# A gated recurrence and a multiplicative FFN on one core: single PSUM banks for the first up product, and a new order

## The chip, the core and the metric

The kernel runs on one core of a Trainium2 chip. The metric is the device time of one execution in microseconds; the median of five runs is given. Five engines matter here: TensorE (PE in the profile; its weight loads are PEld), VectorE (DVE), ScalarE (ACT), GpSimd (POOL), and SyncE (SP), whose queue issues the DMAs. Each takes its instructions in the order in which the program gives them; between engines, semaphores keep the order.

## What is computed

```python
# x, r_gate, i_gate: (4, 5824, 256) f32; a_param: (256,)
a_base = sigmoid(a_param)
a_t    = exp(8 * sigmoid(r_gate) * log(a_base))
norm   = sqrt(max(1 - a_t * a_t, 1e-6))
xg     = norm * sigmoid(i_gate) * x
for t in range(S):                   # a linear recurrence along the sequence
    h = a_t[:, t] * h + xg[:, t]
    y[:, t] = h
# then, over the 23296 rows of y:
out = ((y @ w1) * (y @ w2)) @ w3 @ w_out     # w1, w2: 256x1024, w3: 1024x1024, w_out: 1024x256
```

## The kernel before

The 23296 rows are cut into chunks (`sizes`: one of 256 rows, then 45 of 512). Of each chunk the kernel does the following steps; the letter is the step's name in the string `ORDER`.

- `r`, `i`, `x`: loads, on SP's queue (`load`, L121). `R`, `I`: tanh of half the gates on ACT (L130 or L132, L139), since a sigmoid is (1 + tanh)/2.
- `p`, `t`: (1 + tanh_i) times x on POOL (L144, L160), or fused on DVE (L158).
- `V`, `U`: the r gate and the product u are turned, channels onto partitions: by TensorE with an identity for the chunks in `TURN_R` and `TURN_U` (`turn_pe`, L167, result in PSUM), by a transposing DMA on SP's queue for the others (`turn_dma`, L177).
- `d`, `s`, `q`, `g`: the decay a = exp(...) on ACT in two halves (L188), its square on POOL or DVE (L195), the root on ACT (L199; it needs another activation table than tanh and exp, hence ACT_TABLE_LOAD), and the gating on DVE (L207, L210).
- `h`, `y`: the recurrence, as a hardware scan on DVE per half of the channels (L225), and its cast to bf16 on POOL or DVE (L233).
- `a`, `b`: the two up products on TensorE (`up`, L246). One step `a` makes 256 of the 1024 hidden columns for the chunk's rows: two output groups of 128, one PSUM bank each, held as one tile of two banks. `c`: ACT or DVE copies the tile pa to bf16 in SBUF (L252, L254). `m`: DVE multiplies that copy by pb, which it reads in PSUM (L266).
- `D`: the down product of 128 rows (L277). w3 and w_out were folded into one 1024x256 matrix at the start (`Ft`, `Fc`, `Fm`, `Fe`, L328 to L372). `e`: the output tile, two `D` together, is copied out of PSUM by ACT or DVE (L252, L254). `o`: it is stored, on SP's queue (L296, L292).

[...] `psum` holds three tiles of two banks, which pa and pb take in turn (tag `pab`). `psum_o` holds two single banks, for output tiles, turned gates and folding (tag `po`). A new tile waits for the last reader of the tile whose place it takes.

What runs when is written out by hand in one string: 2037 words such as `a9.3` (step `a`, chunk 9, part 3). A loop at the end of the kernel calls the steps in that order, and each engine's queue is the part of the string that falls to it. Gates run several chunks ahead of the products. Sets of chunk numbers choose the engine of a step that several could do: `DV_COPY`, `DV_EVAC`, `DV_SQUARE`, `DV_CAST`, `DV_TIMES` put it on DVE.

Of the kernel before, what the change touches and what calls it, by code (L numbers as in the profile page):

```python
# [22 lines left out]
def kernel(  # L23
# [26 lines left out]
    sizes = [256] + [CT] * 45  # L50
# [10 lines left out]
    psum = ctx.enter_context(tc.tile_pool(name="psum", bufs=3, space=bass.MemoryType.PSUM))  # L61
    psum_o = ctx.enter_context(tc.tile_pool(name="psum_o", bufs=2, space=bass.MemoryType.PSUM))
# [5 lines left out]
    la4 = consts.tile([P, NCB], F32, tag="la4")  # L68
    zz, zd, zt = (consts.tile([P, NCB], F32, name=tag, tag=tag) for tag in ("zz", "zd", "zt"))
# [9 lines left out]
    TURN_R = {0, 1, 2, 3, 4, 5, 7, 8, 13}  # L79
    TURN_U = {0, 1, 2, 3, 5, 8, 9}  # L80
    DV_TIMES = {0, 1, 2, 8}
    DV_PLUS = set()
    DV_HALF = set()
    DV_SQUARE = {(0, 0), (0, 1), (1, 0), (1, 1), (5, 0), (6, 0), (7, 1), (9, 1), (11, 0), (12, 0), (14, 0), (15, 1),
        (20, 1), (24, 1), (27, 0), (29, 0), (36, 0), (37, 0), (38, 0), (41, 0)}
    DV_CAST = {0, 20, 28, 37, 39, 40, 42, 45}
    DV_COPY = {(0, 3), (1, 1), (1, 3), (2, 1), (3, 2), (7, 2), (8, 0), (8, 1), (10, 0), (11, 1), (13, 0), (14, 0),
        (14, 2), (15, 3), (18, 1), (18, 3), (19, 3), (20, 3), (21, 3), (22, 3), (23, 1), (25, 0), (25, 2), (28, 1), (33,
        1), (33, 2), (36, 3), (40, 2), (41, 2), (41, 3), (44, 0), (45, 0)}
    DV_EVAC = {(0, 0), (1, 1), (2, 0), (2, 1), (3, 0), (4, 0), (4, 1), (5, 0), (6, 1), (7, 1), (8, 1), (9, 1), (10,  # L90
        0), (17, 0), (18, 1), (19, 0), (19, 1), (22, 0), (23, 1), (27, 0), (27, 1), (28, 1), (30, 0), (31, 0), (33, 1),
        (34, 1), (35, 0), (35, 1), (41, 1), (42, 0), (42, 1)}
    FOLD_ACT = {('c', 7), ('e', 0), ('e', 1), ('e', 4), ('e', 6), ('e', 7)}
    W_ACT = {('w2', 0), ('w3', 1), ('w3', 2), ('w3', 3)}
    W_DVE = {('w3', 0)}
    STAGE = {'w1': ['a', 'a'], 'w2': ['nrm', 'nrm'], 'wo': ['a', 'nrm'], 'w3': ['a', 'nrm', 'a', 'nrm', 'a', 'nrm',
        'a', 'nrm']}
    WARM = [30, 30, 24]
    src = {"r": rf, "i": jf, "x": xf}

    def flat(t):
        return t.rearrange("p cb j q -> p (cb j q)").rearrange("p (j d) -> p j d", d=D)

# [22 lines left out]
    def tanh_r(c):  # L126
        n = sizes[c] // P
        t = gates.tile([P, NCB, 4, P], BF16, name="th_r", tag="th_r")
        if c in TURN_R:
            nc.scalar.activation(out=flat(t)[:, :n, :], in_=T["r", c][:, :n, :], func=AF.Tanh, scale=0.5)  # L130
        else:
            nc.scalar.activation(out=t.rearrange("p cb j q -> p j cb q"), in_=cut(T["r", c]),  # L132
                                 func=AF.Tanh, scale=0.5)
        T["thr", c] = t
# [7 lines left out]
    def plus(c):  # L142
        t = T["thi", c]
        (nc.vector if c in DV_PLUS else nc.gpsimd).tensor_scalar(t, t, 1.0, 1.0, op0=ALU.add, op1=ALU.mult)  # L144

    def times(c, half):
# [5 lines left out]
        js = slice(0, n) if fused else slice(2 * half, 2 * half + 2)  # L152
        if c in TURN_U:
            u, t, xt = flat(u)[:, js, :], t[:, js, :], xt[:, js, :]
        else:
            u, t, xt = u.rearrange("p cb j q -> p j cb q")[:, js], cut(t)[:, js], cut(xt)[:, js]
        if fused:
            nc.vector.scalar_tensor_tensor(out=u, in0=t, scalar=1.0, in1=xt, op0=ALU.add, op1=ALU.mult)  # L158
# [15 lines left out]
    def turn_dma(c, key, nm):  # L174
        pool, tag = (gates, "rt") if key == "pr" else (held, "ut")
        dst = pool.tile([P, NCB, 4, P], BF16, name=tag, tag=tag)
        nc.sync.dma_start_transpose(out=dst.rearrange("p cb j q -> p (cb j) q"),  # L177
                                    in_=T[nm, c].rearrange("p cb j q -> p (cb j q)"))
        T[key, c] = dst.rearrange("p cb j q -> p cb (j q)")
# [10 lines left out]
    def square(c, cb):  # L190
# [3 lines left out]
        eng = nc.vector if (c, cb) in DV_SQUARE else nc.gpsimd  # L194
        eng.tensor_mul(out=T["n", c][:, cb, :w], in0=T["a", c][:, cb, :w], in1=T["a", c][:, cb, :w])  # L195
# [18 lines left out]
    def scan(c, cb):  # L214
# [3 lines left out]
        cuts = [0] + [b * S - starts[c] for b in range(1, B) if 0 < b * S - starts[c] < w] + [w]  # L218
        for lo, hi in zip(cuts[:-1], cuts[1:]):
            if (starts[c] + lo) % S == 0:  # L220
                init = 0.0
            else:
                pw = sizes[c - 1]
                init = T["h", c - 1][:, cb, pw - 1:pw]
            nc.vector.tensor_tensor_scan(  # L225
                T["h", c][:, cb, lo:hi], T["a", c][:, cb, lo:hi], T["n", c][:, cb, lo:hi],
                init, ALU.mult, ALU.add)

    def cast(c):
        w = sizes[c]  # L230
        T["y", c] = ypool.tile([P, NCB, CT], BF16, name="y_t", tag="y", bufs=4)
        eng = nc.vector if c in DV_CAST else nc.gpsimd
        eng.tensor_copy(out=T["y", c][:, :, :w], in_=T["h", c][:, :, :w])  # L233

    def warm(i):
        pp = psum.tile([P, 2, CT], F32, name="warm", tag="pab")
# [3 lines left out]
    def up(c, mp, nm, w_sb):  # L240
        w = sizes[c]
        pp = psum.tile([P, 2, CT], F32, name=nm, tag="pab")
        for q in range(2):
            m = 2 * mp + q
            for cb in range(NCB):
                nc.tensor.matmul(out=pp[:, q, :w], lhsT=w_sb[:, cb, m * P:(m + 1) * P],  # L246
                                 rhs=T["y", c][:, cb, :w], start=(cb == 0), stop=(cb == NCB - 1))
        T[nm, c, mp] = pp
# [7 lines left out]
    def copy(c, mp):  # L256
        w = sizes[c]
        sa = ffn.tile([P, 2, CT], BF16, name="sa", tag="sa")
        copy_to((c, mp) in DV_COPY, sa[:, :, :w], T["pa", c, mp][:, :, :w])
        T["sa", c, mp] = sa  # L260
# [54 lines left out]
    def load_w(nm, i):  # L315
        T["wf", nm, i] = held.tile([P, NCB, CT], F32, name="wf", tag=STAGE[nm][i])
# [31 lines left out]

    def rates_abs():
        nc.vector.scalar_tensor_tensor(out=zz, in0=la4, scalar=-1.0, in1=la4, op0=ALU.mult, op1=ALU.min)  # L350
# [23 lines left out]
    def last(c):  # L374
# [8 lines left out]
        "a": lambda c, mp: up(c, mp, "pa", w1_sb), "b": lambda c, mp: up(c, mp, "pb", w2_sb),  # L383
# [8 lines left out]
        "W": warm, "E": cast_ident, "A0.": rates_abs, "A1.": rates_exp, "A2.": rates,  # L392
# [3 lines left out]
        A0. r1 r0 i0 Lw3.0 x0 i1 A1. E R1 R0 x1 V0 V1 Lw1.1 Cw1.1 I0 A2. d0.0 d0.1 d1.0 d1.1 r2 Lw1.0 Lw2.0 Lw2.1 W1  # L396
        I1 s0.0 Cw3.0 s0.1 t0.1 s1.0 s1.1 W0 U0 i2 Cw1.0 q0 t1.1 g0 h0.0 q1 R2 U1 Lw3.1 h0.1 y0 W2 a0.2 g1 h1.0 c0.2
        V2 x2 h1.1 Lwo.1 Cw2.1 Cw2.0 Lwo.0 Ft0 a0.0 r4 a0.1 d2.0 c0.0 Lw3.2 c0.1 r3 b0.0 b0.1 s2.0 m0.0 m0.1 I2 d2.1
        Lw3.5 y1 Fc0 b0.2 b0.3 m0.2 s2.1 Lw3.4 a0.3 c0.3 m0.3 Cw3.1 Cwo.1 a1.2 Ft1 q2 a1.0 t2.1 Cwo.0 U2 i3 a1.1 c1.2
        b1.0 Fc1 c1.0 g2 c1.1 h2.0 R4 h2.1 m1.0 Lw3.3 Fm1 Fm0 Fe1 Fe0 y2 i4 b1.1 Cw3.5 r6 V4 b1.2 m1.1 m1.2 R3 V3 d4.0  # L400
        d4.1 a1.3 Ft5 d3.0 b1.3 a2.0 d3.1 Cw3.2 Fc5 x3 Ft2 c1.3 s4.0 Cw3.4 s4.1 I3 Lw3.6 Lw3.7 r5 s3.0 x4 s3.1 c2.0
        Fc2 p3 t3.0 I4 Cw3.3 Fm5 R6 i5 t3.1 b2.0 m1.3 Fe5 Cw3.6 p4 Fm2 q3 Ft4 a2.2 Fe2 m2.0 Ft3 Fc4 Fc3 a2.1 c2.1 Fm4
        U3 q4 Fe4 g3 a2.3 c2.2 Fm3 Ft6 r7 R5 Fe3 b2.1 Fc6 Cw3.7 Ft7 V6 r9 Fm6 b2.2 m2.1 Fc7 Fe6 c2.3 Fm7 V5 b2.3 x5
        t4.0 t4.1 I5 U4 Fe7 h3.0 h3.1 D1.0 d5.0 d5.1 R7 D1.1 m2.2 e1.0 y3 R9 m2.3 i6 i7 a3.0 g4 D0.0 h4.0 V7 a3.1 h4.1
        a3.2 p5 d6.0 c3.0 c3.1 d7.0 x6 d7.1 V9 r8 b3.0 I6 D0.1 s5.0 d9.0 d9.1 c3.2 y4 m3.0 e0.0 b3.1 d6.1 R8 b3.2 a4.0
        D1.2 r11 D1.3 m3.1 m3.2 s7.0 a4.1 s5.1 t5.0 p6 t5.1 e1.1 s6.0 c4.0 b4.0 s6.1 U5 s7.1 c4.1 I7 b4.1 o1.0 m4.0
        m4.1 q5 D2.0 D2.1 i8 e2.0 a4.2 a3.3 a4.3 q6 c4.2 b4.2 g5 c3.3 r10 r12 D2.2 b4.3 c4.3 b3.3 q7 h5.0 t6.0 p7 D2.3
# [121 lines left out]
```

## Time and profile before

| | us |
|---|---|
| median of 5 runs | 521.53 (519.48 to 522.41) |
| the profiled execution | 519.48 |
| its span | 517.7 |
| TensorE busy | 500.6 |
| VectorE busy | 476.6 |
| ScalarE busy | 429.5 |
| GpSimd busy | 298.4 |

The profile records one execution. Its span runs from the first to the last recorded instruction; the execution's own time is a little longer. A row of a group gives source line, engine, operation, the tiles written and read with shape and type, the count, the busy time, the mean of one in nanoseconds, and behind the second bar the idle time of the engine just before those instructions with what ended it. A row of the timeline begins with start and duration in microseconds; brackets hold the idle time before it and its releaser. Durations of neighbours on one engine can overlap, so the distance between starts is what the next instruction feels. Ends of matmuls are modelled.

### The profile page before, as it was taken

Reading aid. Unit: us, or ns where it says so; the run is one execution under the profiler, and the core shown is the slowest. Engines: PE = TensorE matmul, PEld = TensorE weight load, DVE = VectorE, ACT = ScalarE, POOL = GpSimd, SP = SyncE. Lnnn points to the kernel's source line nnn. Section 1 sums busy time; section 2 is a strip of 40 time slices with the busy share of each in tenths; the row PEclk is TensorE's granted clock in tenths of the full one; section 3 lists DMA queues with packets and bytes.
Section 4 is the critical chain, followed back from the end, with each engine's and each line's share of the span. In section 5 each row is a group of like instructions: output and inputs, shape, how many; then the busy total and the mean of one; then the engine's idle time right before and its main releaser. Section 6 shows DMA issues by size and latency. Waiting matters only on the chain.

```text
span 517.7 us, 8827 instructions
## 1 busy us (share of the span) xinstructions
PE 500.6 (97%) x3260; PEld 308.4 (60%) x3260; DVE 476.6 (92%) x456; ACT 429.5 (83%) x493; POOL 298.4 (58%) x251
## 2 busy tenths in 40 slices
PE   4799999999999999999999999999999999999997
PEld 4567666556565665566665556556556565566555
DVE  4998999999999999899999899999998998999973
ACT  6999998998898988999987997988977797766432
POOL 0677755777828765876566755757357756624000
PEclk9999999999999999999999999999999999999999
DMA  8999989899998876999879978998866978343113
GB/s 298 405 410 311 352 255 255 273 268 275 336 321 205 225 228 186 299 247 302 242 229 296 245 211 220 300 232 241 245 178 210 266 222 205 101 123 83 61 55 109
DMA packets 174604, 123.28 MB, mean 238 GB/s; under 512 B 84448, under 2 KB 170208, under 8 KB 174560
## 3 DMA queue, kind: packets, MB, share of 16 engines
q1 hardware_dynamic: 174288, 122.71, 82.3%
q8 instruction: 25, 0.41, 0.3%
q14 instruction: 19, 0.16, 0.1%
q10 hardware_dynamic: 272, 0.00, 0.0%
HBM read 78.91 MB, written 23.86 MB: 199 GB/s over the span
## 4 chain that ended last, share of the span: by engine, by line
PE 78%; DVE 12%; DMA 4%; issue 4%; POOL 1%; ACT 0%; SPq 0%; DVEq 0%; ACTq 0%; POOLq 0%
PE pb L246 26%; PE po L277 25%; PE pa L246 25%; DVE g_t L266 5%; DVE h_t L225 3%; DMA wf<-in_moe_w_dram 3%; PE pw L342 1%; DVE sa L252 1%; DVE nrm L210 1%; DMA out_dram<-ot 1%; PE ptr L167 1%; PE ptw L331 1%; DVE ot L252 0%; POOL y_t L233 0%; DVE nrm L195 0%
## 5 line engine op out<-in xcount | busy, mean ns | idle before, releaser
L246 PEld LDWEIGHTS <-w_sb 128*128 128x128 bf16 x1472 | 143.0, 98 | 149.8 <-issue 9.3
L266 DVE TENSOR_TENSOR g_t<-sa,pb 128x1024 bf16<-128x1024 bf16 (+1 forms) x184 | 216.0, 1199 | 16.9 <-PE pb L246 12.3
L254 ACT CAST sa<-pa 128x1024 bf16<-128x1024 f32 (+1 forms) x152 | 149.5, 1003 | 50.7 <-PE pa L246 47.3
L246 PE MATMUL pa<-y_t,w_sb 128*128 128x512 bf16 (+1 forms) x736 | 180.4, 377 | 3.1 <-DVE y_t L233 1.2
L246 PE MATMUL pb<-y_t,w_sb 128*128 128x512 bf16 (+1 forms) x736 | 180.1, 377 | 3.2 <-DVE sa L252 1.3
L277 PE MATMUL po<-wp_sb,g_t 128*128 128x256 bf16 x1456 | 179.4, 273 | 0.0
L277 PEld LDWEIGHTS <-g_t 128*128 128x128 bf16 x1456 | 142.3, 98 | 42.5 <-issue 0.2
L225 DVE TENSOR_TENSOR_SCAN h_t<-a_t,h_t,nrm 128x512 f32<-128x512 f32 (+3 forms) x90 | 116.6, 1321 | 1.2
L160 POOL TENSOR_TENSOR u_t<-th_i,x_t 128x512 bf16<-128x512 f32 x84 | 113.6, 1369 | 1.7 <-DMA ut<-u_t 0.8
L233 POOL CAST y_t<-h_t 128x1024 bf16<-128x1024 f32 x38 | 44.4, 1169 | 117.7 <-DVE h_t L225 101.1
L195 POOL TENSOR_TENSOR nrm<-a_t 128x512 f32<-128x512 f32 x72 | 85.0, 1193 | 18.2 <-ACT a_t L188 18.1
L144 POOL TENSOR_SCALAR th_i<-th_i 128x1024 f32<-128x1024 f32 x42 | 48.1, 1148 | 30.7 <-ACT th_i L139 30.7
L188 ACT ACTIVATE a_t<-rt,la 128x512 f32<-128x512 bf16 x74 | 59.1, 818 | 2.6 <-DMA rt<-th_r 1.5
L139 ACT ACTIVATE th_i<-i_t 128x1024 f32<-128x1024 f32 (+1 forms) x46 | 48.3, 1052 | 8.0 <-DMA i_t<-in_i_gate_dram 5.1
L210 DVE SCALAR_TENSOR_TENSOR nrm<-nrm,ut 128x1024 f32<-128x1024 f32 x39 | 52.7, 1354 | 0.7 <-DMA ut<-u_t 0.7
L254 ACT COPY ot<-po 128x512 f32<-128x512 f32 (+1 forms) x60 | 34.6, 577 | 17.2 <-PE po L277 16.2
L199 ACT ACTIVATE nrm<-nrm 128x1024 f32<-128x1024 f32 (+1 forms) x46 | 46.9, 1048 | 0.3
L252 DVE CAST sa<-pa 128x1024 bf16<-128x1024 f32 (+1 forms) x32 | 38.3, 1197 | 5.6 <-PE pa L246 5.4
L132 ACT ACTIVATE th_r<-r_t 128x1024 bf16<-128x1024 f32 x37 | 39.2, 1060 | 0.1
L199 ACT ACT_TABLE_LOAD x20 | 25.7, 1283 | 1.6 <-DVE nrm L195 1.3
L252 DVE COPY ot<-po 128x512 f32<-128x512 f32 (+1 forms) x33 | 21.9, 665 | 4.0 <-PE po L277 4.0
L195 DVE TENSOR_TENSOR nrm<-a_t 128x512 f32<-128x512 f32 (+1 forms) x20 | 17.7, 892 | 0.9 <-ACT a_t L188 0.9
(51 smaller groups left out, 153.3 us busy)
## 6 DMA issues: line engine op xcount, KB each, us to landing
r_t<-in_r_gate_dram SPq DMA_DIRECT2D x45, 512.0 KB, 5.7
i_t<-in_i_gate_dram SPq DMA_DIRECT2D x45, 512.0 KB, 5.3
x_t<-in_x_dram SPq DMA_DIRECT2D x45, 512.0 KB, 5.4
out_dram<-ot SPq DMA_DIRECT2D x89, 256.0 KB, 3.4
wf<-in_moe_w_dram SPq DMA_DIRECT2D x12, 512.0 KB, 9.2
wf<-in_moe_w_out_dram SPq DMA_DIRECT2D x2, 512.0 KB, 10.3
ut<-u_t SPq DMA_TRANSPOSE x39, 4.9
rt<-th_r SPq DMA_TRANSPOSE x37, 4.4
```

The costliest lines, as they stand in the source:

```text
L139: nc.scalar.activation(out=t[:, :n, :], in_=T["i", c][:, :n, :], func=AF.Tanh, scale=0.5)
L160: (nc.vector if (c, half) in DV_HALF else nc.gpsimd).tensor_mul(out=u, in0=t, in1=xt)
L188: nc.scalar.activation(out=a, in_=pr, func=AF.Exp, scale=la4[:, cb:cb + 1], bias=la4[:, cb:cb + 1])
L195: eng.tensor_mul(out=T["n", c][:, cb, :w], in0=T["a", c][:, cb, :w], in1=T["a", c][:, cb, :w])
L199: nc.scalar.activation(out=T["n", c][:, :, :w], in_=T["n", c][:, :, :w], func=AF.Sqrt, scale=-1.0, bias=1.0)
L210: nc.vector.scalar_tensor_tensor(out=T["n", c][:, :, :w], in0=T["n", c][:, :, :w], scalar=1e-3, in1=T["pu", c][:, :, :w], op0=ALU.max, op1 ...
L225: nc.vector.tensor_tensor_scan(T["h", c][:, cb, lo:hi], T["a", c][:, cb, lo:hi], T["n", c][:, cb, lo:hi], init, ALU.mult, ALU.add)
L246: nc.tensor.matmul(out=pp[:, q, :w], lhsT=w_sb[:, cb, m * P:(m + 1) * P], rhs=T["y", c][:, cb, :w], start=(cb == 0), stop=(cb == NCB - 1))
L252: nc.vector.tensor_copy(out=dst, in_=src_ps)
L254: nc.scalar.copy(out=dst, in_=src_ps)
L266: nc.vector.tensor_mul(out=T["g", c][:, 2 * mp:2 * mp + 2, :w], in0=T["sa", c, mp][:, :, :w], in1=T["pb", c, mp][:, :, :w])
L277: nc.tensor.matmul(out=po, lhsT=T["g", c][:, k, j * P:(j + 1) * P], rhs=wp_sb[:, k, :], start=(k == 0), stop=(k == KD - 1), skip_group_che ...
```

## The change

- **PSUM.** pb keeps tiles of two banks, now two of them in a pool of its own. pa becomes a tile of one bank, made and copied in two steps (`a9.3.0`, `a9.3.1`, `c9.3.0`, `c9.3.1`). It shares a ring of four single banks with the output tiles, the turned gates and the folding.
- **Copies.** A copy of pa is 512 columns wide instead of 1024. The product `m` still reads both halves at once.
- **Chunks.** Two chunks of 256 rows at the start, 44 of 512, one of 256 at the end (`dense` keeps small chunks contiguous for the transposing DMA).
- **Scans.** A scan that crosses a batch boundary was cut in two. Now the decay is set to zero at the boundary (`memset`) and one scan runs over it.
- **Engines.** The sets are new: squares may go to ACT (`AC_SQUARE`), casts too (`AC_CAST`); after chunk 10 all copies of pa and after chunk 9 all output copies but one of the last chunk's are on ACT. `TURN_R` and `TURN_U` are smaller.
- **Head.** a_param is loaded as two rows and turned by TensorE (`A3.`); warm-up matmuls (`W`) are regrouped.
- **Order.** A new string of 2452 words.

```diff
-    sizes = [256] + [CT] * 45
+    sizes = [256, 256] + [CT] * 44 + [256]
...
-    psum = ctx.enter_context(tc.tile_pool(name="psum", bufs=3, space=bass.MemoryType.PSUM))
-    psum_o = ctx.enter_context(tc.tile_pool(name="psum_o", bufs=2, space=bass.MemoryType.PSUM))
+    psum_b = ctx.enter_context(tc.tile_pool(name="psum_b", bufs=2, space=bass.MemoryType.PSUM))
+    psum_o = ctx.enter_context(tc.tile_pool(name="psum_o", bufs=4, space=bass.MemoryType.PSUM))
...
-    TURN_R = {0, 1, 2, 3, 4, 5, 7, 8, 13}
-    TURN_U = {0, 1, 2, 3, 5, 8, 9}
+    TURN_R = {0, 1, 2, 3, 4, 7, 12}
+    TURN_U = {0, 1, 2, 3, 6}
...
+    AC_SQUARE = {(1, 0), (2, 0), (3, 0), (4, 1), (7, 0), (10, 0), (11, 0), (12, 1), (13, 0), (13, 1), (14, 0), (14,
+        1), (15, 1)}
+    AC_CAST = {4}
+    DV_EVAC = {(5, 0), (9, 0), (9, 1)}
...
+        if (c, cb) in AC_SQUARE:
+            nc.scalar.activation(out=n, in_=a, func=AF.Square)
...
-        cuts = [0] + [b * S - starts[c] for b in range(1, B) if 0 < b * S - starts[c] < w] + [w]
-        for lo, hi in zip(cuts[:-1], cuts[1:]):
...
+        if cb == 0:
+            for b in range(1, B):
+                if 0 < b * S - starts[c] < w:
+                    nc.vector.memset(a[:, :, b * S - starts[c]:b * S - starts[c] + 1], 0.0)
...
+        nc.vector.tensor_tensor_scan(h[:, cb, :], a[:, cb, :], n[:, cb, :], init, ALU.mult, ALU.add)
...
-    def up(c, mp, nm, w_sb):
-        w = sizes[c]
-        pp = psum.tile([P, 2, CT], F32, name=nm, tag="pab")
+    def up(c, m, dst, w_sb):
+        w = sizes[c]
+        for cb in range(NCB):
+            nc.tensor.matmul(out=dst[:, :w], lhsT=w_sb[:, cb, m * P:(m + 1) * P],
+                             rhs=T["y", c][:, cb, :w], start=(cb == 0), stop=(cb == NCB - 1))
+
+    def up_a(c, mp, q):
+        T["pa", c, mp, q] = pp = psum_o.tile([P, CT], F32, name="pa", tag="po")
+        up(c, 2 * mp + q, pp, w1_sb)
+
+    def up_b(c, mp):
+        T["pb", c, mp] = pp = psum_b.tile([P, 2, CT], F32, name="pb", tag="pb")
         for q in range(2):
...
+            up(c, 2 * mp + q, pp[:, q, :], w2_sb)
...
-    def copy(c, mp):
-        w = sizes[c]
-        sa = ffn.tile([P, 2, CT], BF16, name="sa", tag="sa")
-        copy_to((c, mp) in DV_COPY, sa[:, :, :w], T["pa", c, mp][:, :, :w])
-        T["sa", c, mp] = sa
+    def copy(c, mp, q):
+        w = sizes[c]
+        if q == 0:
+            T["sa", c, mp] = ffn.tile([P, 2, CT], BF16, name="sa", tag="sa")
+        copy_to((c, mp, q) in DV_COPY, T["sa", c, mp][:, q, :w], T["pa", c, mp, q][:, :w])
...
+    def rates_turn():
+        pt = psum_b.tile([P, 2, CT], F32, name="pr_la", tag="pb")
+        nc.tensor.matmul(out=pt[:, 0, :NCB], lhsT=la_rows, rhs=ident_f[:NCB, :NCB], is_transpose=True,
+                         start=True, stop=True)
+        T["la"] = pt[:, 0, :NCB]
```

A stretch of the old order, and then one of the new:

```
D7.0 s12.1 r18 U13 o6.1 V16 I15 g11 D7.1 e7.0 r17 s14.0 m9.1 D7.2 b9.2 p12 s13.1 t12.0 t12.1
```

```
c11.2.0 q13 a11.1.0 q15 c11.1.0 b11.1 b11.0 g13 y12 a11.1.1 a11.2.1 D10.0 D10.1 D10.2 D10.3 c11.1.1 t16.0 a11.3.0
```

## The prediction

> **What bounds the kernel now.** I read the page first, then the three busy engines by stages of 20 us, then TensorE's timeline for its gaps, then ScalarE's for the pitch of its copies.
>
> ```profile
> PE 500.6 (97%) x3260; PEld 308.4 (60%) x3260; DVE 476.6 (92%) x456; ACT 429.5 (83%) x493; POOL 298.4 (58%) x251
> PEclk9999999999999999999999999999999999999999
> L254 ACT CAST sa<-pa 128x1024 bf16<-128x1024 f32 (+1 forms) x152 | 149.5, 1003 | 50.7 <-PE pa L246 47.3
> L254 ACT COPY ot<-po 128x512 f32<-128x512 f32 (+1 forms) x60 | 34.6, 577 | 17.2 <-PE po L277 16.2
> ```
>
> A busy PE need not be PE at its peak, so the 97% decides nothing; the starts in the timeline do:
>
> ```profile
> 16.33 0.60 PE L246 MATMUL pa<-y_t,w_sb 128*128 128x256 bf16 x4 [1.24 <-DVE y_t L233]
> 22.74 1.02 PE L246 MATMUL pa<-y_t,w_sb 128*128 128x512 bf16 x4 [0.62 <-POOL y_t L233]
> ...
> 309.04 1.02 PE L246 MATMUL pa<-y_t,w_sb 128*128 128x512 bf16 x4 [0.61 <-DVE g_t L266]
> 376.80 1.02 PE L246 MATMUL pb<-y_t,w_sb 128*128 128x512 bf16 x4 [1.25 <-DVE sa L252]
> ...
> 482.24 1.03 PE L246 MATMUL pa<-y_t,w_sb 128*128 128x512 bf16 x4
> 483.10 1.04 PE L277 MATMUL po<-wp_sb,g_t 128*128 128x256 bf16 x8
> 483.97 1.03 PE L246 MATMUL pb<-y_t,w_sb 128*128 128x512 bf16 x4
> 507.36 7.15 PE L277 MATMUL po<-wp_sb,g_t 128*128 128x256 bf16 x64
> ```
>
> From 482.24 to 483.10 and to 483.97: four matmuls of 512 columns take 0.866 us of PE, eight of 256 take 0.871. Eight turning matmuls of 128 take 0.445 (first starts of neighbouring groups). The program's useful work is then: first and second up product 315.3 (360 full half-chunk steps of 0.866 and 8 small of 0.436), down product 182 x 0.871 = 158.5, folding 10.6, turned gates 6.7: 491.1 us. The last matmul ends at 514.35 (507.36+7.15, less the 0.16 by which a group's end stands over the next start). So PE loses 23.3 us: 15.0 before 16.33 (1.3 of turns taken off), 2.3 from there to 22.74, and 6.0 later, in some ten gaps that end on VectorE (the two above are the largest). After PE's end come 3.3 us to the span's 517.7.
>
> ```profile
> 0.00:20.00 20.00, 10.98 (x142) 10.05 (x143) 12.97 (x31) 14.99 (x20) 3.88 (x9) 1.00 0.91 338
> 20.00:40.00 20.00, 19.14 (x159) 12.38 (x158) 19.34 (x24) 19.93 (x24) 16.00 (x16) 1.00 1.04 405
> 40.00:60.00 20.00, 19.97 (x157) 13.55 (x156) 18.38 (x21) 19.96 (x27) 13.08 (x12) 1.00 1.12 311
> 200.00:220.00 20.00, 19.80 (x118) 11.31 (x116) 18.34 (x16) 19.07 (x23) 15.37 (x14) 1.00 0.77 222
> 440.00:460.00 20.00, 20.00 (x123) 11.80 (x121) 19.13 (x17) 13.20 (x18) 12.55 (x10) 1.00 0.42 119
> ```
>
> Columns after the length: PE, weight loads, DVE, ACT, POOL. ACT is full from 20 to 60 us, having been idle 5.1 us before 60 (20-14.99, 0.07, 0.04). Later it has slack and DVE hasn't. So TensorE is the bound, and what can be won is 6 us of late gaps, a little head and the turns. ACT's place just behind it in the first 60 us matters for this change.
>
> **The change part by part.**
>
> *Fewer turns.* TURN_R and TURN_U shrink; with two chunks of 256 the turns cost 8 x 0.445 + 4 x 0.22 = 4.4 instead of 6.7. PE's work becomes 488.8: -2.3, all on the bound. In exchange there are 6 more transposing DMAs (82 for 76) on SP's queue, and three more loads. Transposes are late now for 1.5 (ACT on rt) and 0.7 us (DVE on ut) in all, as they are issued chunks ahead; cover gone, 1 us each.
>
> *Smaller banks.* pa is a single bank, four in a ring with po; pb keeps two doubles. Now PE's next product waits for the third tile back of pa and pb alike (fill 0.87, then DVE 1.14 or ACT 0.9). After it, a late DVE blocks only a later pb and a late ACT only the fourth single tile back, some 4 us of PE work. I expect most of the 6.0 us that end on DVE to go; what is late next is ACT. A PE group that waits for its bank holds every later matmul, the turns for ACT's own next decay among them.
>
> *Split copies and work moved from DVE to ACT.* By start-to-start times of neighbours ACT's 1024-column copy costs 0.91 us, a 512-column one 0.48 (ot, mean 0.487 of 42; sa of 512, 0.47 of 3). A pair costs 0.96: +0.05, 9 us over 184 pairs, not the 0.15 that the durations (2 x 577 - 1003) suggest. ACT's copies go from 149 full and 3 small ones to 324 and 11, its output copies from 60 to 88, and it takes 13 squares (not shown before: between 0.48, a copy, and 0.72, the decay of 512; I take 0.62) and one cast. Table loads fall from 40 to 34 behind the first (x 1.29). ACT: 420 -> 458 us. DVE loses 20 full copies' worth of time, 29 output copies, 15 squares and 7 casts: 461 -> 417. Uncut scans: the six pairs of pieces cost 10.8 us in the page's group of 90 against 6 x 1.35 = 8.1, and three memsets of two columns cost 0.2 each by the smallest DVE rows: -2 us of DVE, hidden. SP holds an output store until its copy is done; loads and transposes queue behind it, as they already do. POOL gains 9 us and has 200 to spare. The rates' turn adds one matmul and one DVE copy (0.2 by the small rows) ahead of the first exponential; a wait for the loads hides both, and uncovered they cost 0.5.
>
> *The new order.* Here the sum is decided. Each engine takes its instructions in the order of the ORDER string, so I summed, for every PE step, the ACT work up to the copy that frees its bank, and took off the PE work ahead of it. Before, this lead is at most 10.9 us in the upkeep of the ring (at b3.0: ACT 48.2 up to c3.0, PE 37.5 ahead). It falls below 5 by PE's 120th microsecond. That agrees with the trace: 5.1 idle + 48.2 = 53.3, and b3.0 starts at 55.0, unhindered.
>
> In the new order the lead stands at 14.6 to 15.3 from PE's 20th to its 150th microsecond and is still 12.7 at 200. At its top, D10.2 takes the bank of a11.1.0. ACT up to c11.1.0: 17 R and 15 I x 0.97 = 31.0, 30 d x 0.72 = 21.6, 13 q x 0.97 = 12.6, 13 table loads x 1.29 = 16.8, 48 copies x 0.48 = 23.0, 13 output copies 6.2, 12 squares 7.4, five w3 casts 4.8, small forms and the rest 10.2: 133.6. PE ahead of D10.2: 78 a x 0.433, 38 b x 0.866, 34 D x 0.871, folding 10.6, small ones and turns 11.5: 118.2. With the same 5.1 us of idle ACT at the head (its first gates wait for the same loads; la arriving as two rows instead of 4-byte pieces frees the first exponential earlier, but i1 and r2 then set the start), D10.2 starts at 5.1 + 133.6 + 0.1 = 138.8. Unhindered by ACT it would be 118.2 + 17.3 = 135.5: ACT holds PE back by 3.3 us, once, and nothing later wins it back, PE being full.
>
> *Sum.* 138.8 + (488.8 - 118.2) = 509.4. ACT must stay full for 130 us; from 20 to 60 it lost 0.11 in 40 us, in a stage with room; I allow 1.4. Gaps later: 0.5 instead of 4.5. PE ends at 511.3; with 3.3 to the end (the last chunk's half size changes only what PE covers) the span is 514.6. The profiled execution took 519.48, 1.8 above its span: 516.4, or -3.1. Its time is 2.05 below the median of 521.53, so 518.4 on that scale.
>
> [...] The trace has 0.48 us from one 512-column copy to the next. [...]
>
> **Rivals.**
>
> *ACT is dearer than its neighbours' starts say (slower).* Place: ACT's queue from 20 to 270 us, where copies of half the size stand between waits. Price: 150 copies times the excess. [...] For it: ACT has no slack for half the span, so any excess adds up. Against: 42 pairs at 0.487. Chance 0.29.
>
> *The gain is eaten exactly.* ACT waits inside the full stretch of 3 us more (its waits for PE on sa are 47.3 us now, all outside the full stretch), or DVE's late gaps stay: 521.5. DVE's own lead rises too, from 7.5 to 11.6 (at D8.0), with 7.0 us idle by 20 us: 18.6 against ACT's 20.5, so any DVE scan lengthened by POOL's traffic meets little cover there. Chance 0.16.
>
> *ACT keeps up (faster by more).* If copies cost 0.45 or ACT starts 1.5 us earlier, DVE's 18.6 sets the offset: 1.9 us and half of the slip (0.7) are won, 515.8. Chance 0.15, beside 0.40 for my sum.
>
> **How the numbers follow.** A difference under 0.3% (1.6 us) can't be told from none here. Faster takes my sum and the last rival, 0.55; same 0.16; slower 0.29. Low end: no idle ACT at the head beyond 4 us and no slip, 513.0. High end: the ScalarE rival up to about 0.565 per copy, 528.
>
> **What would show it.** Right: ACT at 19.8 or more of every 20 us from 20 to about 160; PE's gaps in that stretch ending on ACT sa or ot, some 3 to 5 us in all; almost no gap after 250 us; DVE near 430 busy; PE's last matmul near 511. The last rival: gaps there under 2 us. Wrong: start-to-start of sa copies above 0.52; gaps on ACT growing beyond 160 us; PE waiting for rt, ut or y_t; a first up product later than 17.5.

## The result, and the profile after

The changed kernel takes 523.41 us (median of 29 runs, 522.32 to 524.54), the kernel before 520.9 us (50 runs, 519.48 to 524.12). The ratio is 1.0043, 95% interval 1.0033 to 1.0053: by the ratio it is slower by about 2.3 us, where 3.1 us less was forecast. The profiled execution has a span of 521.6 us against 517.7. These 3.9 us are more than the 2.3 mostly because the profiled execution of the kernel before, 519.48 us, is the fastest of its 50, 1.4 us under their median.

The page of the changed kernel, the rows that answer to those of before (engine: busy, share, instructions; group: count, busy, mean ns, idle time before):

```profile
PE 502.6 (96%) x3271; PEld 312.6 (60%) x3271; DVE 442.2 (85%) x425; ACT 467.6 (90%) x716; POOL 317.1 (61%) x262
PEclk8999999999999999999999999999999999999999
L276 ACT CAST sa<-pa 128x512 bf16<-128x512 f32 (+1 forms) x335 | 181.9, 591 | 25.7 <-PE pa L260 21.0
L276 ACT COPY ot<-po 128x512 f32<-128x512 f32 x88 | 51.7, 591 | 17.4 <-PE po L299 16.1
```

VectorE is 34 us less busy over the whole span. The average says nothing on the stage that lost, which the windows show (columns after the length: PE, weight loads, DVE, ACT, POOL, clock, DMA share, GB/s):

```profile
0.00:20.00 20.00, 13.98 (x151) 12.86 (x152) 11.74 (x34) 14.72 (x22) 2.78 (x9) 0.83 0.92 337
20.00:40.00 20.00, 16.31 (x142) 11.61 (x142) 18.85 (x36) 18.10 (x24) 15.54 (x15) 1.00 1.11 379
40.00:60.00 20.00, 18.04 (x153) 12.55 (x152) 19.37 (x24) 19.97 (x30) 11.43 (x11) 1.00 0.95 294
80.00:100.00 20.00, 19.44 (x128) 12.09 (x127) 19.40 (x20) 19.91 (x29) 12.58 (x10) 1.00 1.10 306
100.00:120.00 20.00, 18.17 (x114) 10.93 (x112) 19.89 (x19) 17.31 (x25) 11.98 (x9) 1.00 1.03 257
200.00:220.00 20.00, 20.00 (x126) 12.16 (x125) 16.89 (x13) 19.34 (x33) 16.34 (x13) 1.00 1.08 278
440.00:460.00 20.00, 20.00 (x125) 12.04 (x124) 15.99 (x15) 19.17 (x32) 12.62 (x10) 1.00 0.46 123
```

At 200 and at 440 us TensorE is full and VectorE has 3 to 4 us of slack: there the change did what it was to do. From 40 to 120 us VectorE is as full as ever, and from 100 to 120 it is ScalarE that idles (17.31). TensorE's timeline, changed kernel, names who ended its gaps:

```profile
17.48 0.38 PE L260 MATMUL pa<-y_t,w_sb 128*128 128x256 bf16 x2
...
32.40 1.03 PE L370 MATMUL pw<-wo_sb,w3t 128*128 128x256 bf16 x8 [1.35 <-DVE sa L274]
...
59.75 1.02 PE L260 MATMUL pb<-y_t,w_sb 128*128 128x512 bf16 x4 [0.89 <-DVE g_t L288]
...
99.00 0.59 PE L260 MATMUL pa<-y_t,w_sb 128*128 128x512 bf16 x2 [0.56 <-DVE ot L274]
...
105.17 1.02 PE L260 MATMUL pb<-y_t,w_sb 128*128 128x512 bf16 x4 [1.01 <-DVE g_t L288]
...
109.52 1.91 PE L299 MATMUL po<-wp_sb,g_t 128*128 128x256 bf16 x16 [0.73 <-DVE sa L274]
```

From 57 to 120 us the larger gaps end on VectorE, not on ScalarE; before that they end on VectorE, ScalarE and GpSimd in turn. The gaps (the distance between the starts of neighbouring matmuls, less the work of the first at the prediction's 0.866, 0.871 and 0.445 us for a group; a gap counts where it ends) compare as follows:

| stretch | before | after |
|---|---|---|
| first up product at | 16.33 | 17.48 |
| gaps from there to 40 us | 2.3 | 5.1 |
| 40 to 80 us | 0.2 | 3.5 |
| 80 to 120 us | 1.1 | 3.2 |
| after 120 us | 4.8 | 1.7 |

With the turns (-2.3 us of work) the differences sum to 1.15 + 2.8 + 3.3 + 2.1 - 3.1 - 2.3 = 3.95, against 3.9 of span. The late gaps are won as forecast. The first 120 us cost 9 us.

What held TensorE at 109.52 is seen in VectorE's timeline:

```profile
100.82 3.19 DVE L241 TENSOR_TENSOR_SCAN h_t<-a_t,h_t,nrm 128x512 f32<-128x512 f32 x2
103.93 2.32 DVE L288 TENSOR_TENSOR g_t<-sa,pb 128x1024 bf16<-128x1024 bf16 x2
106.17 0.72 DVE L170 TENSOR_TENSOR u_t<-th_i,x_t 128x512 bf16<-128x512 f32 x1
106.81 2.05 DVE L224 SCALAR_TENSOR_TENSOR nrm<-nrm,ut 128x1024 f32<-128x1024 f32 x1
108.78 0.68 DVE L274 CAST sa<-pa 128x512 bf16<-128x512 f32 x1
```

No idle time stands between these rows: the copy that frees the bank (108.78) is late because of what lies ahead of it in the queue. Two scans take 3.19 where two take 2.46 at 76.80, and the gating 2.05 where it takes 1.21 at 82.03. While TensorE waits, ScalarE has no pa to copy, as its timeline shows:

```profile
107.09 0.58 ACT L276 CAST sa<-pa 128x512 bf16<-128x512 f32 x1 [1.68 <-PE pa L260]
```

### The profile page after: what moved, and what is told of

It reads as the page before. It is cut to its first block, busy times and chain, and to the rows that moved or that the text cites. A ratio compares the mean times of both kernels' runs of the same rounds, so it can differ in the third digit from the quotient of the medians.

```text
span 521.6 us, 9063 instructions
## 1 busy us (share of the span) xinstructions
PE 502.6 (96%) x3271; PEld 312.6 (60%) x3271; DVE 442.2 (85%) x425; ACT 467.6 (90%) x716; POOL 317.1 (61%) x262
## 4 chain that ended last, share of the span: by engine, by line
PE 74%; DVE 4%; ACT 4%; issue 2%; DMA 1%; SPq 0%; DVEq 0%; ACTq 0%
PE po L299 26%; PE pb L260 25%; PE pa L260 24%; DVE g_t L288 1%; DVE h_t L241 1%; DMA i_t<-in_i_gate_dram 1%; ACT sa L276 1%; DVE nrm L224 1%; ACT a_t L199 1%; ACT ot L276 1%; DVE sa L274 0%; ACT th_r L139 0%; ACT nrm L213 0%; DVE u_t L170 0%; ACT L199 0%
## 5 line engine op out<-in xcount | busy, mean ns | idle before, releaser
L276 ACT CAST sa<-pa 128x512 bf16<-128x512 f32 (+1 forms) x335 | 181.9, 591 | 25.7 <-PE pa L260 21.0
L250 POOL CAST y_t<-h_t 128x1024 bf16<-128x1024 f32 (+1 forms) x45 | 55.8, 1239 | 130.4 <-DVE h_t L241 121.9
L241 DVE TENSOR_TENSOR_SCAN h_t<-a_t,h_t,nrm 128x512 f32<-128x512 f32 (+1 forms) x92 | 128.7, 1420 | 1.3
L170 POOL TENSOR_TENSOR u_t<-th_i,x_t 128x512 bf16<-128x512 f32 (+1 forms) x85 | 121.1, 1439 | 4.9 <-DMA x_t<-in_x_dram 1.7
L209 POOL TENSOR_TENSOR nrm<-a_t 128x512 f32<-128x512 f32 (+1 forms) x76 | 88.9, 1181 | 22.3 <-ACT a_t L199 22.1
L276 ACT COPY ot<-po 128x512 f32<-128x512 f32 x88 | 51.7, 591 | 17.4 <-PE po L299 16.1
L199 ACT ACTIVATE a_t<-rt,la 128x512 f32<-128x512 bf16 (+1 forms) x80 | 64.5, 824 | 0.3 <-DMA rt<-th_r 0.2
L224 DVE SCALAR_TENSOR_TENSOR nrm<-nrm,ut 128x1024 f32<-128x1024 f32 (+1 forms) x42 | 58.2, 1387 | 2.7 <-ACT nrm L213 2.7
L151 POOL TENSOR_SCALAR th_i<-th_i 128x1024 f32<-128x1024 f32 (+1 forms) x44 | 49.4, 1123 | 15.9 <-ACT th_i L146 15.9
L139 ACT ACTIVATE th_r<-r_t 128x1024 bf16<-128x1024 f32 (+1 forms) x40 | 42.7, 1068 | 0.0
```

Source lines behind the costliest of these rows:

```text
L170: (nc.vector if (c, half) in DV_HALF else nc.gpsimd).tensor_mul(out=u, in0=t, in1=xt)
L199: nc.scalar.activation(out=a, in_=pr, func=AF.Exp, scale=la4[:, cb:cb + 1], bias=la4[:, cb:cb + 1])
L209: (nc.vector if (c, cb) in DV_SQUARE else nc.gpsimd).tensor_mul(out=n, in0=a, in1=a)
L224: nc.vector.scalar_tensor_tensor(out=T["n", c][:, :, :w], in0=T["n", c][:, :, :w], scalar=1e-3, in1=T["pu", c][:, :, :w], op0=ALU.max, op1 ...
L241: nc.vector.tensor_tensor_scan(h[:, cb, :], a[:, cb, :], n[:, cb, :], init, ALU.mult, ALU.add)
L276: nc.scalar.copy(out=dst, in_=src_ps)
```

## The experiments

Theory after the result: up to about 110 us the queues of VectorE and ScalarE together pace the kernel, and VectorE's is the later one. Rivals: the copies cost more for being halved, the ring itself stalls, ScalarE's load in the head, the small chunks at the start, or work that simply comes late on GpSimd.

### The kernel before, with halved copies

```diff
-        copy_to((c, mp) in DV_COPY, sa[:, :, :w], T["pa", c, mp][:, :, :w])
+        for q in range(2):
+            copy_to((c, mp) in DV_COPY, sa[:, q, :w], T["pa", c, mp][:, q, :w])
```

> The kernel before, with each copy of pa made in two halves of one bank; nothing else. Front theory (the loss of the changed kernel lies in its first 110 us, where the new order and sets fill ACT and DVE; a split copy costs 0.05 us more of ACT, 0.03 of DVE per pair): +0 to +1.5 us against before, as ACT has room. Ring theory (the finer copies themselves cost): each pair 0.15 us dearer on ACT and 0.2 on DVE, +3 us or more.

521.83 us, ratio to before 1.0007 (0.9988 to 1.0025). Halved copies cost nothing that can be measured, in a kernel whose ScalarE is full for 40 us and whose VectorE is full for much longer. In the changed kernel a 512-column copy on ScalarE is followed after 0.477 us by the next instruction (median of the 252 copies with no idle time behind them, mean 0.475), where 0.48 was taken.

### The new banks under the old order

The kernel before with both pools of the change and the halved copies; its own chunks, sets and order, of whose 2405 words 146 were brought forward.

```diff
-    psum = ctx.enter_context(tc.tile_pool(name="psum", bufs=3, space=bass.MemoryType.PSUM))
-    psum_o = ctx.enter_context(tc.tile_pool(name="psum_o", bufs=2, space=bass.MemoryType.PSUM))
+    psum_b = ctx.enter_context(tc.tile_pool(name="psum_b", bufs=2, space=bass.MemoryType.PSUM))
+    psum_o = ctx.enter_context(tc.tile_pool(name="psum_o", bufs=4, space=bass.MemoryType.PSUM))
```

> The kernel before with only the new PSUM rings and split copies: old chunks, sets and order, each a and c in two steps, and a reader brought forward in the order where the ring of four or the two pb would otherwise wait for a later word (146 of 2405 words). Front theory: the first 110 us lose at most 2 us, late gaps shrink from 4.5 to 2 or less: -3 to +3 us against before. Ring theory: gaps on ACT sa/ot and DVE g_t all along the span, +6 us or more.

582.85 us, 1.1178 (1.1147 to 1.1209). Rows of its waits (engine and tile waiting, releaser: us in all, times, longest):

```profile
ACT ot L259 <- PE po L282: 43.9, 27, 5.6
PE pb L243 <- DVE g_t L271: 19.9, 17, 3.4
```

With two tiles for pb the product `b` waits for `m` 17 times, from 24 to 568 us, 19.9 us in all. That is a third of the 62 us; how much of the rest came from the ring of four and how much from moving the 146 words stays open. The banks and the order can't be judged apart by this run: under the old order this ring is far slower.

### ScalarE relieved: its squares to GpSimd

```diff
-    AC_SQUARE = {(1, 0), (2, 0), (3, 0), (4, 1), (7, 0), (10, 0), (11, 0), (12, 1), (13, 0), (13, 1), (14, 0), (14,
-        1), (15, 1)}
+    AC_SQUARE = set()
```

> The changed kernel with its 13 ACT squares on POOL. If ACT is what paces the first 150 us (7 us less for it there): -3 to -6 us against the changed kernel. If DVE paces them, or the head's waits do: within 1 us of it. If POOL's latency on the way from decay to root matters more: slower.

526.72 us, 1.0106 (1.0079 to 1.0133): 3.3 us above the changed kernel, not below it. Lines of TensorE's timeline:

```profile
60.81 1.02 PE L259 MATMUL pb<-y_t,w_sb 128*128 128x512 bf16 x4 [1.90 <-DVE g_t L287]
...
110.88 1.91 PE L298 MATMUL po<-wp_sb,g_t 128*128 128x256 bf16 x16 [0.73 <-DVE sa L273]
...
153.46 0.59 PE L259 MATMUL pa<-y_t,w_sb 128*128 128x512 bf16 x2 [0.98 <-POOL y_t L249]
```

The same product `b` that waited 0.89 us now waits 1.90, and later the casts of y on GpSimd, behind the added squares, are late. The wait at 109.52 is here at 110.88 with the same 0.73 us, so ScalarE's relief did not shorten it. The edit mixes ScalarE's relief with later squares, so it doesn't show that ScalarE's load costs nothing.

### VectorE relieved

```diff
-    DV_PLUS = {2}
-    DV_HALF = {(5, 0), (5, 1), (8, 0), (9, 0), (11, 0)}
+    DV_PLUS = set()
+    DV_HALF = set()
```

> The changed kernel with five half products and one plus moved from DVE to POOL (chunks 2 to 11, some 4 us less for DVE before 110 us). If DVE paces the first 110 us: -2 to -4 us against the changed kernel. If ACT does: within 1 us. If POOL's traffic slows DVE's scans more: slower.

521.02 us, 0.9988 (0.9977 to 0.9999): by the ratios 0.55% or 2.9 us below the changed kernel (2.3 us by the spans, 519.3 against 521.6). Five half products at 0.66 to 1.21 us, started between 53.9 and 106.2 us, and one `p` at 0.68 went to GpSimd, 4.6 us in all. Its windows:

```profile
80.00:100.00 20.00, 19.89 (x130) 12.44 (x131) 19.76 (x20) 19.91 (x29) 15.80 (x12) 1.00 1.10 314
100.00:120.00 20.00, 19.85 (x124) 12.14 (x125) 19.90 (x19) 19.94 (x30) 12.87 (x10) 1.00 1.06 263
```

Against 18.17 and 17.31, TensorE and ScalarE are now full from 100 to 120 us: the gaps at 99.00, 105.17 and 109.52 are gone. ScalarE's idle time there had been TensorE's wait for VectorE, passed on. The relief brings the kernel back to the level of before, 2.9 of the 5.4 us by which the forecast missed; it doesn't bring the gain.

### The same, and twelve copies moved from VectorE to ScalarE

The kernel of the experiment before this, without the twelve copies that `DV_COPY` has for chunks 7 to 10:

```diff
-        ... (7, 3, 0), (7, 3, 1), (8, 1, 0), (8, 1, 1), (9, 0, 1), (9, 1, 1), (9, 2, 1), (9, 3, 0), (10, 0, 0), (10, 1, 0),
+        ...
```

> The changed kernel with the six POOL moves of the DVE relief and, besides, the twelve DVE copies of chunks 7 to 10 moved to ACT (+6 us of ACT, -8 us of DVE before 120 us). If DVE was the only pacer up to 110 us: -1 to -2 us against the DVE relief alone. If ACT's lead in the order is the next limit, as the prediction counted: +2 to +6 us against the DVE relief alone, with PE's gaps between 80 and 130 us ending on ACT sa or ot.

528.02 us, 1.0113 (1.0075 to 1.0151), 6.5 us above the kernel that it was made from. A row of its waits (26.9 us in the kernel that it was made from) and rows of TensorE's timeline:

```profile
DVE g_t L284 <- ACT sa L272: 41.6, 39, 4.1
```

```profile
120.14 1.03 PE L295 MATMUL po<-wp_sb,g_t 128*128 128x256 bf16 x8 [0.84 <-ACT sa L272]
...
143.33 1.02 PE L256 MATMUL pb<-y_t,w_sb 128*128 128x512 bf16 x4 [2.58 <-DVE g_t L284]
```

Twelve copies at 0.48 are 5.8 us of ScalarE, and they come out as 6.5. With VectorE relieved, ScalarE's lead is the next limit: the two stand within a few us of each other.

### VectorE relieved, and ScalarE relieved of the w3 casts

```diff
-    W_ACT = {('w3', 1), ('w3', 3), ('w3', 4), ('w3', 5), ('w3', 6)}
+    W_ACT = set()
```

> The changed kernel with the DVE relief and the five w3 casts of ACT (31 to 46 us) on POOL. If ACT's load in the head causes the gaps there (6.5 us from 17 to 40 us): -1 to -3 us against the DVE relief alone. If the head is held by DVE and by the one ring that turns, folding and pa share: within 1 us of it.

522.95 us, 1.0018 (1.0003 to 1.0034): 1.6 us worse than with VectorE relieved alone. GpSimd does the casts later (the last starts at 46.1 us, on ScalarE at 44.9), and a product waits 1.69 us at 61.06 for VectorE again. Relief and delay are mixed here too: moving these casts to GpSimd doesn't help, but what ScalarE's load in the head costs stays open.

### Late relief of VectorE in the kernel before

The copies and output copies from chunk 17 on, except those of 44 and 45, go to ScalarE in the kernel before.

```diff
-         (14, 2), (15, 3), (18, 1), (18, 3), (19, 3), (20, 3), (21, 3), (22, 3), (23, 1), (25, 0), (25, 2), (28, 1), (33,
-         1), (33, 2), (36, 3), (40, 2), (41, 2), (41, 3), (44, 0), (45, 0)}
+         (14, 2), (15, 3), (44, 0), (45, 0)}
```

> The kernel before, its old PSUM tiles and order, with DVE's copies and output copies of the late chunks (17 and on, but 44 and 45) on ACT. If the late gaps of before were only a late DVE, this wins them without a ring: -2 to -4 us against before. If they came from the double tiles that pa and pb share: within 1 us, or slower where ACT's place in the order is wrong.

534.98 us, 1.0249 (1.0209 to 1.0288). TensorE's timeline has gaps such as these:

```profile
223.77 1.04 PE L242 MATMUL pa<-y_t,w_sb 128*128 128x512 bf16 x4 [2.00 <-ACT sa L250]
...
254.20 1.86 PE L242 MATMUL pa<-y_t,w_sb 128*128 128x512 bf16 x4 [2.63 <-ACT sa L250]
```

The late gaps can't be won by moving these copies in the old order. The changed kernel has nearly all of them on ScalarE and only 1.7 us of late gaps; whether its banks or its order bring that was not separated.

### Uncut scans alone, in the kernel before

```diff
-        cuts = [0] + [b * S - starts[c] for b in range(1, B) if 0 < b * S - starts[c] < w] + [w]
-        for lo, hi in zip(cuts[:-1], cuts[1:]):
...
+                    nc.vector.memset(a[:, :, b * S - starts[c]:b * S - starts[c] + 1], 0.0)
...
+        nc.vector.tensor_tensor_scan(h[:, cb, :], a[:, cb, :], n[:, cb, :], init, ALU.mult, ALU.add)
```

> The kernel before with uncut scans only (three memsets for six scan pieces; 2 us less of DVE at chunks 11, 23 and 34). Every theory: -0.5 to 0 us, hidden; more only if DVE is late just there.

520.11 us, 0.9977 (0.9966 to 0.9988): 1.2 us faster than before, and faster than both kernels. The gap that the prediction's lines have at 376.80, 1.25 us on VectorE's copy, is 0.41 here:

```profile
377.01 1.02 PE L246 MATMUL pb<-y_t,w_sb 128*128 128x512 bf16 x4 [0.41 <-DVE sa L252]
```

The memset takes 0.06 us at 370.11 of VectorE's timeline. The prediction and the expectation called this part hidden; 0.84 us of it lay in one of the few late gaps.

### The folding left out, in the kernel before and in the changed one

Both leave out the folding of w3 and w_out (10.6 us of TensorE, with its copies); the folded matrix is a constant, filled by GpSimd.

```diff
+    nc.gpsimd.memset(wp_sb, 0.03)
...
-    ... Ft0 ... Fc0 ... Fm0 ... Fe0 ...      (all words of the folding, in ORDER)
```

> The kernel before without its folding of w3 and w_out: the 32 folding steps are left out and the folded weights are a constant, so the output is another; loads and casts of the weights stay. Both theories: PE has 10.6 us less work, DVE 6, ACT 2.5; about -10 us against before. It is the base for the next run.

> The changed kernel without the folding, in the same way. If the head is slow because folding, turns and pa share one ring (waits on another step's late reader): the gaps from 17 to 45 us fall from 6.5 to under 3, and it comes out at or below the kernel before without folding. If the head is slow for the small chunks and for DVE and ACT being full: it stays 2 us or more behind it, as with the folding.

The kernel before falls to 520.31 us, 0.9976 (0.9965 to 0.9988), by 1.3 us and not by 10. The changed one falls to 521.36 us, 0.9987 (0.997 to 1.0005), by 2.9 us of ratio. The windows of the kernel before without folding (the last three columns are the granted clock, the DMA share and GB/s):

```profile
20.00:40.00 20.00, 15.56 (x92) 7.45 (x90) 18.12 (x19) 19.70 (x23) 14.26 (x14) 1.00 1.04 407
40.00:60.00 20.00, 16.73 (x102) 9.31 (x103) 15.91 (x16) 18.71 (x23) 13.85 (x13) 0.91 1.04 294
```

TensorE is not the bound in the first 60 us even of the kernel before: taken away, its folding leaves gaps that end on GpSimd (4.1 us), VectorE (2.6) and ScalarE (2.4). The folding had filled time in which TensorE would have waited. One thing blurs this: from 43.2 to 46.6 us, after two such gaps, the matmuls of 512 columns start 0.43 us apart instead of 0.217, and the granted clock of that window is 0.91. That can have cost 1.7 us of the missing 9.

In the changed kernel without folding the gaps up to 60 us grow from 7.8 to 16.4 us, where a shared ring as the cause would have brought them under 3. The time stays some 0.6 us of ratio behind the kernel before without folding, between the two outcomes that were named, so the run decides neither. Some 6 us of these gaps are matmuls at half their rate (32.0 to 37.9 and 45.5 to 51.5 us, granted clock 0.83 from 20 to 40 and from 40 to 60). The three gaps on VectorE at 96.31, 102.47 and 106.82 stay (0.56, 1.01, 0.73 us of wait), just as they are with folding. Without the folding VectorE has twelve copies less, 6.8 us by their durations, all before 55 us, and no more than 2.9 us came out: VectorE's work so early did not count in full.

### Small chunks at both ends, in the kernel before

```diff
-    sizes = [256] + [CT] * 45
+    sizes = [256, 256] + [CT] * 44 + [256]
```

> The kernel before, old PSUM tiles and order, with the chunk sizes of the changed one (256, 256, 44 times 512, 256; the last chunk's steps simply put at the end, where they cost up to 6 us that are not looked at). Looked at: PE's first product and its gaps up to 60 us. If small first chunks alone cost the head: first product and gaps from 17 to 60 us worse than before by 3 us or more. If not: the first product at 16 us or earlier and gaps there within 1 us of before's 2.6.

531.15 us, 1.0181 (1.0156 to 1.0206); the last small chunk's steps stand at the very end of the old order, so that time says nothing on the tail of the changed kernel. Its head does:

```profile
15.54 0.60 PE L246 MATMUL pa<-y_t,w_sb 128*128 128x256 bf16 x4 [1.74 <-DVE y_t L233]
...
24.20 0.62 PE L167 MATMUL ptr<-ident,u_t 128*128 128x128 bf16 x8 [1.16 <-DVE u_t L158]
```

The first product comes earlier than in both kernels, so two small chunks don't delay it. But the gaps from there to 60 us are 5.8 us, 2.5 in the kernel before. Start and gaps together, this head is 2.5 us behind the kernel before at 60 us, and the changed kernel's is 6.4 behind. The expectation had set 3 us as the sign of small chunks and 1 us as the sign against them: as a part of the late head they are not ruled out.

### VectorE relieved, and a shorter head

```diff
-    WARM = [26, 16, 24, 36]
+    WARM = [26, 16, 24, 8]
...
-        ... V3 a0.1.1 d3.0 I2 d3.1 c0.1.1 ...
+        ... V3 a0.1.1 d3.0 d3.1 c0.1.1 I2 ...
```

> The changed kernel with the DVE relief, 28 warm-up matmuls fewer just ahead of the first product ([...]end 0.5 us after y is there), and tanh_i of chunk 2 put behind the decay of chunk 3, whose turned tile the product a0.3.0 waits for in the ring. If such waits set the head: -0.5 to -1.2 us against the DVE relief alone. If later DVE and ACT work sets the pace in any case: within 0.3 us.

520.86 us, 0.9988 (0.9978 to 0.9998): the same ratio as without this edit. The first product starts at 16.37 us, at 17.93 with VectorE relieved alone and at 17.48 in the changed kernel, and nothing of that is left at the end. An earlier start of TensorE is worth nothing here. The runs did not show the expectation's "half clock" for the matmuls left out: with VectorE relieved the last 37 ahead of the product take 2.15 us, from 15.78 to 17.93, which is 0.058 each, where slow ones of the changed kernel start 0.106 us apart.

### More work on VectorE, early and late

Three kernels, each the changed kernel with six more half products on VectorE (4.1 us by its own five, 0.69 each at the median):

```diff
-    DV_HALF = {(5, 0), (5, 1), (8, 0), (9, 0), (11, 0)}
+    DV_HALF = {..., (6, 0), (6, 1), (7, 0), (7, 1), (9, 1), (10, 0)}          early
+    DV_HALF = {..., (22, 0), (23, 0), (24, 0), (25, 0), (26, 0), (27, 0)}     late
+    DV_HALF = {..., (22, 0), (23, 0), (25, 0), (25, 1), (26, 0), (27, 0)}     late, without the one that waits
```

> The changed kernel with six more half products (chunks 6, 7, 9, 10; some 0.68 us each by the five that VectorE has) moved from GpSimd to VectorE, all before about 110 us: 4.1 us more of VectorE there. Theory (VectorE's queue paces the stretch up to 110 us, so that its work there is paid one for one): 3 to 5 us slower than the changed kernel, gaps of TensorE in 40 to 120 us up by that and ending on VectorE. Rival (GpSimd's late results pace it, and what was gained by taking VectorE's half products away was some other thing): no change or faster, since GpSimd loses 7.6 us of work.

> The changed kernel with one half product of each of chunks 22 to 27 moved from GpSimd to VectorE: the same 4.1 us more of VectorE, but after about 150 us, where it has 1 to 3 us of slack in every 20. Theory (only the stretch up to 110 us is paced by VectorE): within 0.5 us of the changed kernel. Rival (VectorE's load counts wherever it lies): 2 to 4 us slower, with gaps of TensorE ending on VectorE in 150 to 260 us.

> As the run before (six half products more on VectorE after 200 us), but the half product of chunk 24, before which VectorE stood idle for 3.67 us until GpSimd's th_i, stays on GpSimd and the second half of chunk 25 is taken instead. VectorE's work is the same. Theory (late work on VectorE is covered; the loss of the run before came from that one wait, which held the products m queued behind it): within 0.5 us of the changed kernel. Rival (the load itself counts late too): 1.5 to 2.5 us slower than the changed kernel, as before.

Early: 526.32 us, 1.0109 (1.0093 to 1.0124), by the ratios 3.4 us above the changed kernel. TensorE's timeline has the loss in the stretch where it had waited before; these two waits were 0.89 us, and 0.64 us one step earlier, without the edit:

```profile
61.23 1.02 PE L260 MATMUL pb<-y_t,w_sb 128*128 128x512 bf16 x4 [1.88 <-DVE g_t L288]
...
76.82 1.91 PE L299 MATMUL po<-wp_sb,g_t 128*128 128x256 bf16 x16 [1.60 <-DVE sa L274]
```

Late: 525.27 us, 1.0084 (1.007 to 1.0098), 2.1 us above the changed kernel, where nothing was expected. VectorE's and TensorE's timelines show one place:

```profile
250.28 0.69 DVE L170 TENSOR_TENSOR u_t<-th_i,x_t 128x512 bf16<-128x512 f32 x1 [3.67 <-POOL th_i L151]
```

```profile
252.15 1.02 PE L260 MATMUL pb<-y_t,w_sb 128*128 128x512 bf16 x4 [0.80 <-DVE g_t L288]
```

The half product of chunk 24 stood at the head of VectorE's queue for 3.67 us until GpSimd had th_i, and the products `m` behind it stood as well. With that one left on GpSimd and another in its place: 523.34 us, 1.0048 (1.0032 to 1.0065), 0.3 us from the changed kernel, which lies within this interval. So 4.1 us of VectorE's work cost 3.4 us before 110 us and nothing that can be measured after 200; a wait in its queue costs there too.

## Why the prediction was wrong

*Right: the price of a copy.* ScalarE's halved copies are followed after 0.475 us on average; the trace's 0.48 held. The mean duration of one, 591 ns, is longer than that distance, as it was for the output copies of the kernel before (577 ns and 0.487 us). No run shows the 0.565 us per copy from which the high end of the forecast, 528, comes; what they show in its place is the 0.475. The rival that gave the slower side for this reason is out, although the kernel is slower.

*Right: TensorE's and ScalarE's work, and the late gaps.* The turns came as forecast. ScalarE's busy time grew by 38.1 us, where 38 was counted, and the late gaps fell from 4.8 to 1.7 us. VectorE's busy time fell by 34.4 us where 44 was counted, so its sum was the one that was 10 us short.

*Wrong: "ACT holds PE back by 3.3 us, once", with "the same 5.1 us of idle ACT" and 1.4 for its slip.* The sum rested on ScalarE alone from 20 to 160 us. Its idle time up to 140 us was 11.4 us, not 6.5. Of it 2.69 us lie between 100 and 120 us, where TensorE waited for VectorE, and only 0.06 is left of them when VectorE is relieved; 1.9 between 20 and 40 us and 1.1 between 60 and 80 stay. At D10.2, the step on which the sum rested, TensorE did not wait for ScalarE:

```profile
145.08 3.66 PE L299 MATMUL po<-wp_sb,g_t 128*128 128x256 bf16 x32
```

```profile
145.55 1.08 ACT L276 CAST sa<-pa 128x512 bf16<-128x512 f32 x2
```

The four down products of chunk 10 run without a gap; D10.2, the third, starts at 146.8, where 138.8 was forecast, and ScalarE's copy c11.1.0, the first of the two at 145.55, is done 0.7 us before. So ScalarE was close, but the waits that had delayed this step were earlier ones.

*The term that was mis-sized is VectorE's lead.* The prediction gave it 11.6 us of queue and 7.0 of idle time, "18.6 against ACT's 20.5", and left it to a rival. Take the wait at 109.52, the down product D5.2, which needs the copy c7.3.1. At the mean distances of the trace of before, with the fourteen smallest instructions left out, VectorE's queue up to that copy is 94.7 us, so with 7.0 idle it should end at 101.7. It ended at 109.4: 98.6 of work and 10.8 of idle time, 7.7 us later, and the span came out 7.0 above the forecast. Of the 7.7:

- 3.8 are idle time beyond the 7.0: 1.3 before 20 us (8.3 in all), 1.1 from 20 to 40 and 1.4 after that;
- 2.3 are fourteen small instructions of 0.16 to 0.17 us for the rates of a_param, which this count leaves out;
- 1.6 are, in the balance, dearer instructions. Four places alone, at 55.10, 93.01, 100.82 and 106.81 us, where GpSimd works beside a scan or a gating, take 3.2 us more than 1.21 for each of their five instructions; other rows came out a little cheaper than their units.

The last was named in the rival "the gain is eaten exactly" ("any DVE scan lengthened by POOL's traffic meets little cover there"), with a chance of 0.16 and no gain or loss as its outcome. That rival had part of the mechanism; the idle time and the small instructions, 6.1 of the 7.7 us, no rival had.

*Wrong: TensorE as the bound of the head.* The prediction read 97% busy with care but still built on TensorE "being full" after 17 us. Without the folding's 10.6 us the kernel before is only 1.3 us faster, so even there the other engines set the pace of the first 60 us.

*Wrong in small: the head and the scans.* The first product came at 17.48 us, at the edge that the text had named (17.5), but an earlier one brought nothing: the late kernel without the wait has the same head, its first product starts at 16.59, and its time is that of the changed kernel. "-2 us of DVE, hidden" for the uncut scans was 1.2 us of time won.

Shown by the runs: half products on VectorE between about 54 and 110 us cost more than half of their own size in both directions (2.9 us won for 4.6 taken away, 3.4 lost for 4.1 added), and after 200 us they cost nothing where they don't wait.

Not shown: what makes the head late. At 60 us the changed kernel is already 6.4 us behind the kernel before, and relief of VectorE later on left that as it was. The small chunks, the order and the loads are all left as causes. Open too is why VectorE's idle time grew by 3.8 us; its largest single waits are for a load of x (3.8 us) and for the identity (1.3 us).

## What to carry to other kernels

Sum the lead of every engine that comes near the bound, not of the nearest alone, with each instruction of its queue in the sum, however small; a second engine 2 us behind the first is inside the error of such a sum, which was 7.7 us here. An engine that idles while the bound waits may be a victim of a third one: relieve the suspect by a known amount and see whether the time follows, and add work at two places to learn where it counts. Work moved to a queue brings its waits along, and in a queue that keeps its order one wait of 3.7 us can cost more than 4.1 us of work that is covered: with the wait the late kernel was 2.1 us above the changed one, without it 0.3.

## What the runs showed of the hardware

- In the changed kernel's trace, the full-size scans (512 columns) and gatings (1024) take 1.26 us on average (64 of them, at most 1.29) where no GpSimd instruction overlaps them, and 1.60 (66, median 1.57, up to 2.28) where one does. A pair of rows, VectorE's and GpSimd's:

```profile
93.01 2.28 DVE L224 SCALAR_TENSOR_TENSOR nrm<-nrm,ut 128x1024 f32<-128x1024 f32 x1
```

```profile
91.27 5.16 POOL L170 TENSOR_TENSOR u_t<-th_i,x_t 128x512 bf16<-128x512 f32 x3
```

  The gating takes 1.07 us more than the 1.21 at 82.03. Of GpSimd's three the first, over before the gating begins, takes 1.27, the next two 1.72 and 2.25, so both sides are longer. By what mechanism was not shown: no run here took GpSimd's share away alone.
- The 60 warm-up matmuls ahead of the first product took 4.42 us in the changed kernel's profile: 21 start 0.106 us apart, up to 15.2 us, the others 0.056. In the kernel before, the first 17 of its 84 start 0.106 us apart, up to 10.2 us, the rest 0.056. In the late kernel without the wait the 60 last 3.51 us, none of them slow; there they end by 15.7 us, and the first product waits for y instead (0.91 us). The granted clock of the first 20 us is 0.83 in the changed kernel's profile and 1.00 in that of the kernel before: that row did not show the slow matmuls of the second.
- In both kernels without folding, stretches of 3 to 6 us with matmuls at half their rate come after gaps of TensorE: 1.9 and 1.1 us before the one at 43.2, waits of 2.3 and 3.1 us before those at 32.0 and 45.5. In the two kernels with folding no such stretch follows the first product: the up products' matmuls of 512 columns start 0.216 us apart there.
- Moving small work (a w3 cast, a square) from ScalarE to GpSimd made the kernel slower by 1.6 and 3.3 us although GpSimd is only 61% busy. In the second case y_t came late from it by 0.98 us at 153.46; the share of busy time said nothing about that.
- ScalarE's table loads take 1.283 us each. Behind the first, 20 of the 39 in the kernel before stand at the root's line (L199) and 19 at those of tanh and the decay; in the changed kernel there are 33.
- The load of a_param moved 272 packets in the kernel before and 4 in the changed one, where it comes as two rows. The exponential of the rates starts at 2.79 us instead of 5.48, but the first decay at 7.92 instead of 7.96.
- SP's queue waited for ScalarE's output copies, ahead of the stores: 91.8 us in the kernel before (25 waits, the longest 10.4) and 73.0 in the changed one (26, the longest 7.3).
